# K and Q of the first three chunks in runs of four tokens, turned by f32 identity matmuls, and a new order for the opening

## The chip, the cores and the metric

The kernel runs on one core of a Trainium2 chip. The core has five engines, each with a list of instructions of its own: TensorE (PE, matmuls; its weight loads are shown as PEld), VectorE (DVE), ScalarE (ACT), GpSimd (POOL) and SyncE (SP), which here only issues DMAs. The engines meet through semaphores. Data comes from DRAM into SBUF (128 partitions) by DMA (the page counts 16 DMA engines and shows five queues); matmuls write to PSUM, which the kernel uses as eight banks of 2 KB per partition. The metric is the device time of one execution in microseconds (us), as the median of several runs; lower is better.

## The reference, cut to what matters

Attention with a window of 128 and 4 sink tokens, over 4 batches, 8 heads, 768 tokens and head size 64, then a feed-forward layer that takes the maximum of three products:

```python
scores = (q @ k.T) / sqrt(64)                 # per batch and head
keep = is_sink | ((rel >= 0) & (rel < 128))   # rel = query position - key position
a = exp(where(keep, scores, -1e9) - max); a = a / sum(a)
x = (a @ v)                                   # heads side by side: 3072 x 512
h = maximum(maximum(x @ w1, x @ w2), x @ w3)  # 512 -> 768
out = h @ w_out                               # 768 -> 512, float32
```

## The kernel before, in words

The 3072 tokens are cut into 12 chunks of 256, three to a batch (`CPB = 3`). Eight heads make four pairs (`NP = 4`); two heads of a pair lie on the two halves of the 128 partitions. Every chunk passes these stages, each a small function that is called by name:

- `load` (L76) brings Q, K or V of a chunk in f32 with one DMA on SP. Partition p gets tokens 2p and 2p+1 of all eight heads, so that one run in DRAM is two tokens of one head, 512 bytes. `gate` is a tiny write by POOL into the target that the DMA has to wait for: `pool_gate` writes at once, in POOL's order; `after(wi, c)` copies one number out of weight `wi`, so it waits until that weight has landed, and POOL with it.
- `cast_qk` (L95) casts half of the pairs (group g) to bf16 on a chosen engine, `cast_v` (L104) a quarter of V.
- `turn` and `turn2` (L109, L129) bring the head size onto the partitions: four transposes on TensorE into a bf16 PSUM tile, then one copy to `kT` or `qT` by ScalarE or VectorE. In `turn2`, K and Q of a group share one PSUM bank. From chunk 4 on `turn_dma` does it with DMA transposes on SP. `qT` and `kT` keep even and odd tokens apart (index i), which the masks allow for.
- `premask` writes a mask into a score bank by a matmul, before `score` adds K times Q for a pair; `expo` takes the exponential on ScalarE; `mask` multiplies on VectorE where there was no `premask`. `sink_k`, `sink_v` and `sink_score` do the four sink tokens; `av_open` opens the output banks, `av` multiplies by V and normalises on VectorE, `xpose` (or `xpose_dma`) turns the result.
- `ffn_h(chunk, fp, wi)` is eight matmuls for a third of the hidden size and one of the three weights, followed by a copy (ScalarE, wi = 0) or a maximum (VectorE); `ffn_y` is the last product, `store` the output in runs of two rows (4 KB).
- `load_w` and `load_wo` load the weights from POOL, cast to bf16 on the way. `warm` issues matmuls on zeros whose result nobody uses.

`bank` takes the first of a list of free PSUM banks and `give` puts it at the end, in the order in which the program is written. So a stage can wait for a bank that an earlier one has not yet emptied. Raw tiles have two buffers for each of Q, K and V.

The order is written out by hand: L454 to L655 are the opening, in which chunks 0 to 3 are brought up and the feed-forward of chunks 0 to 2 is woven in, and L656 to L764 are the main loop, in which the feed-forward of chunk i runs beside the attention of chunk i + 1. Every engine takes its instructions in the order of this list. The first `ffn_h` stands at L536.

Of the kernel before, what the change touches and what calls it, by code (L numbers as in the profile page):

```python
# [16 lines left out]
def kernel(  # L17
# [13 lines left out]
    nc = tc.nc  # L31
# [17 lines left out]
    with tc.manual_schedule():  # L49
# [17 lines left out]
        RING = 4  # L67
        kT = [const.tile([128, 2, NP, 2, 64], BF16, name=f"kT{i}") for i in range(RING)]
# [7 lines left out]
        def load(ci, what="kqv", gate=None, part=None, parts=1):  # L76
# [4 lines left out]
            for w in what:  # L81
# [4 lines left out]
                if gate is not None:  # L86
                    gate(dst[0:1, 0, 0, 0:1])
                n = H // parts
# [6 lines left out]
        def cast_qk(ci, w, g, eng):  # L95
# [4 lines left out]
            f = eng.copy if eng is nc.scalar else eng.tensor_copy  # L100
            f(x[:, 2 * g:2 * g + 2].rearrange("q p i a d -> q p a i d"),  # L101
# [7 lines left out]
        def turn(ci, w, g, eng=None):  # L109

            pt = bank([128, 4, 128], BF16, "pt")
# [16 lines left out]

        def turn2(ci, w, g, eng=None):  # L129

            if w == "k":
                pts[ci, g] = bank([128, 2, 4, 128], BF16, "pt")
# [206 lines left out]
        def av(ci, p):  # L339
# [16 lines left out]
            if p == 0:  # L356
# [7 lines left out]
        def xpose(ci, t, eng=None):  # L364
            eng = eng or nc.scalar
            if t == 0:
# [87 lines left out]
        warm(6)  # L454
        load(0, 'k')
        load(0, 'q', gate=pool_gate)
        warm(6)
        masks()
        premask(0, (2,))
        load(0, 'v', gate=pool_gate)  # L460
        cast_qk(0, 'k', 0, nc.gpsimd)
        sink_init()
        cast_qk(0, 'k', 1, nc.vector)
        premask(0, (3,))
        cast_qk(0, 'q', 0, nc.scalar)
        cast_qk(0, 'q', 1, nc.vector)
        turn2(0, 'k', 0, nc.scalar)
        load(1, 'k')
        premask(0, (0,))
        turn2(0, 'k', 1, nc.scalar)  # L470
        turn2(0, 'q', 1, nc.scalar)
        turn2(0, 'q', 0, nc.vector)
        score(0, (0,))
        expo(0, 0)
        load(1, 'q')
        premask(0, (1,))
        sink_k(0)
        cast_v(0, 1, 1, nc.vector)
        load_w(0, 0, 768)
        score(0, (1,))  # L480
        score(0, (2,))
        warm(3)
        cast_qk(1, 'k', 0, nc.vector)
        cast_v(0, 0, 0, nc.vector)
        cast_v(0, 1, 0, nc.gpsimd)
        expo(0, 2)
        expo(0, 1)
        load(1, 'v')
        av_open(0)
        load_w(1, 512, 768)  # L490
        score(0, (3,))
        cast_v(0, 0, 1, nc.vector)
        cast_qk(1, 'q', 1, nc.gpsimd)
        cast_qk(1, 'k', 1, nc.vector)
        av(0, 0)
        expo(0, 3)
        cast_qk(1, 'q', 0, nc.vector)
        turn2(1, 'k', 0, nc.vector)
        load_w(1, 0, 512)
# [156 lines left out]
        for i in range(3, NCH):  # L656
            n, m = i + 1, i - 1
            more = n < NCH
            if i == 3 or i >= NCH - 2:
# [6 lines left out]
                if more:  # L666
                    sink_score(n)
# [140 lines left out]
```

## Time and profile before

| what | us |
|---|---|
| median of 3 runs (179.58 to 180.5) | 179.67 |
| span of the profiled execution, from its first to its last instruction | 179.1 |
| TensorE busy in the span | 170.6 |
| VectorE busy | 125.3 |
| ScalarE busy | 84.6 |
| GpSimd busy | 61.7 |
| first `ffn_h` matmul starts | 18.50 |
| last `ffn_h` of the opening ends, main loop begins | 58.07 |

The page gives no other time for the profiled execution than its span; the 0.57 us between span and median lie outside the first and last instruction. The granted clock of TensorE reads 1.000 over the whole span.

In rows of the timeline the columns are start, duration, engine, line of the kernel, operation, output tile `<-` input tiles, shape, count; the bracket gives the idle time of the engine just before and what ended it. In rows of groups, the numbers behind the bar are busy time, mean ns of one, and idle time before. In rows of windows, behind the length stand the busy times of PE, PEld, DVE, ACT and POOL, with counts of instructions that touch the window, then the granted clock, the busy share of the DMA engines (it can exceed 1 where packets overlap) and GB/s. Bytes of the weights are counted as written, in bf16.

### The profile page before, as it was taken

What the parts mean: (1) busy time and instruction counts of PE and PEld (TensorE: products, weight loads), DVE (VectorE), ACT (ScalarE), POOL (GpSimd) and SP (SyncE); (2) the same over time, 40 slices, a digit from 0 to 9 for tenths busy, and PEclk for the clock granted to TensorE, in tenths of its full rate; (3) what the DMA queues carried; (4) which work ended last, traced back from release to release, by engine and by line L of the source; (5) the groups of instructions that cost most, each with busy time, mean ns of one, the idle gap of its engine ahead of it and who ended that gap; (6) DMA issues with size and microseconds to landing.
All of it is one profiled execution on the core that took longest, in us unless ns stands there. A gap on an engine that the chain in (4) does not pass through costs nothing.

```text
span 179.1 us, 4647 instructions
## 1 busy us (share of the span) xinstructions
PE 170.6 (95%) x1873; PEld 126.8 (71%) x1873; DVE 125.3 (70%) x271; ACT 84.6 (47%) x169; POOL 61.7 (34%) x121
## 2 busy tenths in 40 slices
PE   7789999979999999999999999999999999999991
PEld 2445889746688588598597597696796795796870
DVE  3189752799699797677676775874875875976451
ACT  3386734853772921931824914914716716420210
POOL 4378630161565395066055055146135000000000
PEclk9999999999999999999999999999999999999999
DMA  4999999979999999995998999998999505202203
GB/s 137 290 288 206 249 212 260 225 196 287 326 186 207 294 206 237 226 276 133 243 273 181 249 193 238 239 198 222 262 157 266 40 20 161 117 6 58 117 0 117
DMA packets 69029, 34.90 MB, mean 195 GB/s; under 512 B 26512, under 2 KB 67472, under 8 KB 69008
## 3 DMA queue, kind: packets, MB, share of 16 engines
q1 hardware_dynamic: 64912, 31.33, 81.2%
q0 software_dynamic: 3952, 3.15, 11.1%
q8 instruction: 14, 0.23, 0.5%
q10 hardware_dynamic: 144, 0.13, 0.2%
q14 instruction: 7, 0.06, 0.1%
HBM read 25.17 MB, written 6.29 MB: 176 GB/s over the span
## 4 chain that ended last, share of the span: by engine, by line
PE 86%; DVE 5%; DMA 4%; POOL 1%; issue 1%; ACT 0%; SPq 0%; POOLq 0%
PE h_ps L390 51%; PE y_ps L411 17%; PE o L350 6%; PE st L274 6%; DMA k_raw<-in_k_dram 4%; DVE e_sb L292 2%; PE xt L371 1%; PE pt L115 1%; PE o L332 1%; DVE vb L105 1%; PE sk L300 1%; PE y_ps L421 1%; DVE h_sb L401 1%; DVE k_bf L101 1%; PE pt L137 0%
## 5 line engine op out<-in xcount | busy, mean ns | idle before, releaser
L390 PE MATMUL h_ps<-xT,w 128*128 128x256 bf16 x864 | 101.9, 273 | 0.2 <-DVE h_sb L401 0.2
L390 PEld LDWEIGHTS <-w 128*128 128x128 bf16 x864 | 81.7, 98 | 10.5 <-issue 0.8
L401 DVE TENSOR_TENSOR h_sb<-h_sb,h_ps 128x512 bf16<-128x512 bf16 (+1 forms) x74 | 49.2, 670 | 17.9 <-PE h_ps L390 16.0
L286 ACT ACTIVATE e_sb<-st 128x512 bf16<-128x512 f32 (+1 forms) x96 | 46.2, 578 | 6.4 <-PE st L274 6.3
L397 ACT CAST h_sb<-h_ps 128x512 bf16<-128x512 f32 x36 | 21.1, 587 | 49.2 <-PE h_ps L390 49.0
L105 POOL CAST vb<-v_raw 64x512 bf16<-64x512 f32 x40 | 26.3, 657 | 28.3 <-DMA v_raw<-in_v_dram 24.8
L411 PE MATMUL y_ps<-wo,h_sb 128*128 128x512 bf16 x138 | 32.7, 380 | 1.0 <-DVE h_sb L401 1.0
L292 DVE TENSOR_TENSOR e_sb<-e_sb,msk 128x1024 bf16<-128x1024 bf16 (+1 forms) x42 | 28.9, 720 | 1.5 <-ACT e_sb L286 1.3
L101 POOL CAST k_bf<-k_raw 128x512 bf16<-128x512 f32 x17 | 11.4, 689 | 40.2 <-issue 23.6
L411 PEld LDWEIGHTS <-h_sb 128*128 128x128 bf16 x138 | 12.4, 98 | 15.6 <-DVE h_sb L401 2.0
L358 DVE TENSOR_TENSOR x_sb<-o,rc 128x256 bf16<-128x256 f32 x48 | 20.4, 424 | 1.6
L413 DVE COPY y_sb<-y_ps 128x512 f32<-128x512 f32 x13 | 9.0, 690 | 13.9 <-PE y_ps L411 13.8
L350 PE MATMUL o<-vb,e_sb 128*128 128x65 bf16 x352 | 17.2, 194 | 0.3 <-DVE vb L105 0.2
L350 PEld LDWEIGHTS <-e_sb 128*128 128x128 bf16 x352 | 14.9, 98 | 2.6 <-DVE vb L105 0.4
L274 PE MATMUL st<-qT,kT 64*128 64x128 bf16 (+1 forms) x256 | 14.5, 238 | 0.6 <-DVE qT L141 0.6
L274 PEld LDWEIGHTS <-kT 64*128 64x128 bf16 x256 | 8.3, 94 | 8.1 <-issue 6.2
L355 DVE RECIPROCAL rc<-o 128x4 f32<-128x4 f32 x48 | 8.4, 176 | 4.2 <-PE o L350 4.1
L101 POOL CAST q_bf<-q_raw 128x512 bf16<-128x512 f32 x17 | 10.1, 619 | 3.0 <-DMA q_raw<-in_q_dram 3.0
L413 ACT COPY y_sb<-y_ps 128x512 f32<-128x512 f32 x10 | 5.9, 586 | 7.6 <-PE y_ps L411 7.4
L306 ACT ACTIVATE e_sink<-sk 128x256 bf16<-128x256 f32 x8 | 3.1, 383 | 12.4 <-PE sk L300 12.4
L177 PE MATMUL warm<-wz 128*128 128x512 bf16 x15 | 5.7, 552 | 1.2 <-DVE wz L166 1.2
L101 DVE CAST q_bf<-q_raw 128x512 bf16<-128x512 f32 x5 | 2.6, 525 | 4.6 <-DMA q_raw<-in_q_dram 4.6
(70 smaller groups left out, 72.2 us busy)
## 6 DMA issues: line engine op xcount, KB each, us to landing
k_raw<-in_k_dram SPq DMA_DIRECT2D x12, 512.0 KB, 5.0
q_raw<-in_q_dram SPq DMA_DIRECT2D x12, 512.0 KB, 6.3
v_raw<-in_v_dram SPq DMA_DIRECT2D x12, 512.0 KB, 7.4
out_dram<-y_sb SPq DMA_DIRECT2D x11, 512.0 KB, 3.3
w<-in_moe_w_dram POOLq DMA_DIRECT2D x4, 256.0 KB, 9.0
w<-in_moe_w_dram POOLq DMA_DIRECT2D x1, 768.0 KB, 8.3
wo<-in_moe_w_out_dram POOLq DMA_DIRECT2D x1, 768.0 KB, 11.0
w<-in_moe_w_dram POOLq DMA_DIRECT2D x1, 512.0 KB, 9.2
```

Of the source, the lines that this page charges most:

```text
L101: f(x[:, 2 * g:2 * g + 2].rearrange("q p i a d -> q p a i d"), y[:, 4 * g:4 * g + 4].rearrange("q (p a) i d -> q p a i d", a=2))
L105: eng.tensor_copy(vb[ci % RING][64 * i:64 * i + 64, n, :, 0:D], raws[ci, "v"][64 * n:64 * n + 64, :, i])
L274: nc.tensor.matmul(st[a][:, s:s + q1 - q0].rearrange("q n (i r) -> q n i r", i=2), lhsT=x[hp, n, p].rearrange("q i r -> q (i r)"), rhs=qc[ ...
L286: nc.scalar.activation(e[:, a, lo:], st[a][:, lo:], AF.Exp, scale=scale)
L292: (eng or nc.vector).tensor_mul(e[:, :, lo:], e[:, :, lo:], msk0 if lo else msk)
L350: nc.tensor.matmul(o[:, t, a], lhsT=e[:, a, s], rhs=vb[cv % RING][:, n, 2 * p + a], start=first, stop=True, skip_group_check=True)
L358: nc.vector.tensor_mul(xs[ci][:, :, p], o[:, :, :, 0:D], rc.unsqueeze(3).to_broadcast([128, 2, 2, D]))
L390: nc.tensor.matmul(hp[:, f].rearrange("q (i t r) -> q i t r", i=2, t=2), lhsT=w_sb[wi][:, ds, c0:c0 + 128], rhs=xTs[ci][:, :, ds].rearrang ...
L397: nc.scalar.copy(dst, hp)
L401: nc.vector.tensor_max(dst[:, x], dst[:, x], hp[:, x])
L411: nc.tensor.matmul(yp, lhsT=hs[ci][:, fb, t * 128:(t + 1) * 128], rhs=wo[:, fb], start=(fb == 0), stop=(fb == FB - 1))
L413: (nc.scalar.copy if eng is None else eng.tensor_copy)(ys[ci][:, t], yp)
```

## The change: what it does

For chunks 0 to 2 (`QUAD = 3`, the whole first batch) K and Q are loaded by two DMAs each. DMA x brings heads 4x to 4x+3 onto the partitions 2p + x, four tokens to a partition, so that a run in DRAM is four tokens of one head, 1024 bytes. `cast_qk` reads the other layout. `turn` and `turn2` hand over to `turn4`: four matmuls against the identity, whose outputs go into an f32 PSUM tile with steps in the address, so that the tokens come out in the layout that `kT` and `qT` had before, and then one copy. Each turn has a bank of its own. V, and Q and K from chunk 3 on, are as before.

The opening is the same set of calls in another order, with other engines for some of the casts and copies, and with 8 and 5 warm matmuls in place of 6, 6 and 3. In the new list every one of the first eight turns copies on ScalarE, `masks_late` comes early on POOL, Q of chunk 1 is loaded ahead of K, the last third of w2 right behind that of w1 and ahead of the rest of w1. The main loop is written in four branches without the tests on `more`. `av` and `xpose` allocate their tile at whichever call comes first.

```diff
+        QUAD = 3
@@ in load
+                if ci < QUAD and w != "v":
+                    for x in range(2):
+                        nc.sync.dma_start(
+                            out=dst.rearrange("(p x) h i d -> x p (h i d)", x=2)[x]
+                                .rearrange("p (h e) -> p h e", h=4),
+                            in_=src[b, 4 * x:4 * x + 4, t0:t0 + 256]
+                                .rearrange("h (p i) d -> p h (i d)", i=4))
+                    continue
@@ in cast_qk
+            if ci < QUAD:
+                f(x[:, 2 * g:2 * g + 2].rearrange("q u v a d -> q (u v) a d"),
+                  y[:, 4 * g:4 * g + 4].rearrange("q (a u) v d -> q (u v) a d", a=2))
+                return
@@ in turn and turn2
+            if ci < QUAD:
+                return turn4(ci, w, g, eng)
@@ new
+        def turn4(ci, w, g, eng=None):
+            pt = bank([128, 2, 2, 2, 32, 2], F32, "pt")
+            x = bfs[ci, w]
+            for i in range(4):
+                y = x[:, 2 * g + i // 2, i % 2].rearrange("s a d -> s (a d)")
+                if w == "q":
+                    o = pt[:, :, i % 2, :, :, i // 2].rearrange("q x n r -> q n r x")
+                else:
+                    o = pt[:, :, :, i % 2, :, i // 2].rearrange("q x n r -> q n r x")
+                nc.tensor.matmul(o, lhsT=y, rhs=ident, start=True, stop=True)
+            eng = eng or (nc.scalar if w == "q" else nc.vector)
+            f = eng.copy if eng is nc.scalar else eng.tensor_copy
+            if w == "q":
+                f(qT[ci % RING].rearrange("q (x p) i n r -> q p x (i n r)", x=2)[:, g],
+                  pt.rearrange("q x i n r j -> q x (i n r j)"))
+            else:
+                f(kT[ci % RING].rearrange("q n (x p) i r -> q p x n (i r)", x=2)[:, g],
+                  pt.rearrange("q x n i r j -> q x n (i r j)"))
+            give(pt)
```

The new list, up to the main loop, on one line for each few calls (calls on several engines, in program order):

```python
load(0,'k'); load(0,'q',gate=pool_gate); masks(); load(0,'v',gate=pool_gate); warm(8); premask(0,(3,))
cast_qk(0,'k',1,nc.scalar); sink_init(); cast_qk(0,'k',0,nc.gpsimd); turn2(0,'k',0,nc.scalar); load(1,'q')
turn2(0,'k',1,nc.scalar); masks_late(); premask(0,(1,)); load_w(0,0,768); cast_qk(0,'q',1,nc.vector)
load(1,'k'); cast_qk(0,'q',0,nc.vector); turn2(0,'q',1,nc.scalar); turn2(0,'q',0,nc.scalar)
score(0,(1,)); score(0,(3,)); load_w(1,512,768); load_w(2,512,768); load(1,'v'); premask(0,(0,))
cast_v(0,1,0,nc.vector); score(0,(0,)); expo(0,1); expo(0,3); load_w(1,0,512); cast_v(1,1,0,nc.gpsimd); warm(5)
...
premask(0,(2,)); av_open(0); expo(0,0); cast_qk(1,'q',1,nc.scalar); cast_qk(1,'q',0,nc.vector); score(0,(2,))
expo(0,2); sink_k(0); cast_qk(1,'k',0,nc.vector); turn2(1,'q',0,nc.scalar); cast_qk(1,'k',1,nc.vector); av(0,3)
sink_v(0); turn2(1,'k',0,nc.scalar); load(2,'k',gate=after(0,300)); av(0,1); av(0,2); load_w(2,0,256)
turn2(1,'q',1,nc.scalar); load(3,'q',gate=after(0)); turn2(1,'k',1,nc.scalar); av(0,0); score(1,(2,)); score(1,(0,))
expo(1,2); cast_qk(2,'q',0,nc.gpsimd); mask(1,2); premask(1,(1,)); load(2,'v',gate=after(1)); xpose(0,0,nc.scalar)
load_w(2,256,512); expo(1,0); score(1,(1,)); load_wo(); xpose(0,1,nc.vector); ...; sink_score(1); score(1,(3,))
expo(1,1); ffn_h(0,2,0); mask(1,0); expo(1,3); ffn_h(0,0,0); cast_qk(2,'k',1,nc.gpsimd); av_open(1)
cast_v(2,1,1,nc.gpsimd); cast_v(2,1,0,nc.gpsimd); load(3,'k',gate=after(1)); av(1,2); av(1,0); av(1,1); av(1,3)
load(3,'v',gate=after(2)); ffn_h(0,1,0); ffn_h(0,2,1); ...; cast_qk(3,'q',1,nc.gpsimd); load(4,'q',gate=pool_gate)
...
turn(2,'k',1,nc.vector); turn(2,'k',0,nc.scalar); ffn_h(0,0,1); sink_score(2); score(2,(2,)); score(2,(0,)); expo(2,2)
cast_qk(3,'q',0,nc.scalar); score(2,(1,)); score(2,(3,)); mask(2,2); expo(2,1); ffn_h(1,0,2); mask(2,1); ffn_h(1,2,2)
expo(2,0); ffn_h(1,1,1); ffn_h(0,1,2); turn(3,'q',1,nc.scalar); expo(2,3); mask(2,0); ffn_h(1,1,2); cast_v(2,0,1,nc.gpsimd)
av_open(2); cast_qk(3,'k',0,nc.gpsimd); cast_qk(3,'k',1,nc.gpsimd); turn(3,'q',0,nc.scalar); load(4,'v')
load(5,'k',gate=pool_gate); av(2,2); mask(2,3); av(2,0); ffn_y(1,0,nc.vector); ffn_y(0,0); turn(3,'k',0,nc.scalar)
...
expo(3,1); load(4,'k',gate=after(2)); ...; store(0); ...; load(5,'q'); ...; turn_dma(4,'q'); turn_dma(4,'k')
...
```

More of the change, by code (lines that the diff above doesn't have):

```diff
@@ L656 @@
         for i in range(3, NCH):
             n, m = i + 1, i - 1
[L658 to L661 removed]
+            if i == 3:
+                sinks(n)
                 load(i + 3)
```

539 lines of the change are left out of this document (294 added, 245 removed).

## The prediction

> **What bounds the kernel now.** I read the page's header and chain first, then the busy windows of its stages, then the timeline of the entry, then what moved the DMA.
>
> ```profile
> span 179.1 us, 4647 instructions
> PE 170.6 (95%) x1873; PEld 126.8 (71%) x1873; DVE 125.3 (70%) x271; ACT 84.6 (47%) x169; POOL 61.7 (34%) x121
> ...
> PE 86%; DVE 5%; DMA 4%; POOL 1%; issue 1%; ACT 0%; SPq 0%; POOLq 0%
> ```
>
> The chain is TensorE nearly everywhere, so time can be won only where TensorE idles or does filler. The windows say where that is.
>
> ```profile
> 0.00:18.50 18.50, 15.09 (x152) 7.86 (x152) 11.24 (x36) 10.51 (x22) 11.68 (x33) 1.00 1.04 230
> 18.50:58.07 39.57, 38.23 (x448) 30.44 (x448) 30.47 (x66) 22.00 (x44) 15.75 (x33) 1.00 1.13 239
> 58.07:164.80 106.73, 106.73 (x1198) 79.97 (x1198) 77.61 (x161) 49.96 (x100) 34.31 (x56) 1.00 0.94 189
> ...
> L177 PE MATMUL warm<-wz 128*128 128x512 bf16 x15 | 5.7, 552 | 1.2 <-DVE wz L166 1.2
> ```
>
> Cuts: the first `ffn_h` starts at 18.50, the main loop at 58.07. The loop is 100% busy to 164.8 and its work is untouched, so a shift of its start passes through to the end. Lost are 18.50 - 15.09 = 3.4 us of idle and 5.7 us of warm matmuls before 18.50 (**entry**), and 39.57 - 38.23 = 1.34 us after it (**middle**). At most these 10.5 us can be won, and some 5 of them pass before K has landed at all.
>
> The entry, from the timeline (start, duration, engine, line, count, in brackets the idle time before it and its releaser):
>
> ```profile
> 0.75 0.46 SPq L90 DMA_DIRECT2D k_raw<-in_k_dram  x1
> 1.20 4.90 PE L177 MATMUL warm<-wz 128*128 128x512 bf16 x12 [1.20 <-DVE wz L166]
> 5.08 0.43 DVE L101 CAST k_bf<-k_raw 128x512 bf16<-128x512 f32 x1 [1.31 <-DMA k_raw<-in_k_dram]
> 5.19 0.79 POOL L101 CAST k_bf<-k_raw 128x512 bf16<-128x512 f32 x1 [2.23 <-DMA k_raw<-in_k_dram]
> 6.58 0.39 PE L137 MATMUL pt<-ident,k_bf 128*128 128x128 bf16 x4
> 6.89 0.43 DVE L101 CAST q_bf<-q_raw 128x512 bf16<-128x512 f32 x1 [1.38 <-DMA q_raw<-in_q_dram]
> 6.95 0.62 ACT L101 CAST q_bf<-q_raw 128x512 bf16<-128x512 f32 x1 [4.70 <-DMA q_raw<-in_q_dram]
> 7.47 1.06 ACT L144 COPY kT<-pt 128x512 bf16<-128x512 bf16 x2
> 8.59 0.61 PE L137 MATMUL pt<-ident,q_bf 128*128 128x128 bf16 x8 [1.07 <-ACT kT L144]
> 9.24 0.90 POOL L239 DMA_DIRECT2D w<-in_moe_w_dram  x1
> 10.14 3.29 ACT L286 ACTIVATE e_sb<-st 128x384 bf16<-128x384 f32 x8 [0.55 <-PE st L274]
> 12.41 0.70 POOL L101 CAST q_bf<-q_raw 128x512 bf16<-128x512 f32 x1 [0.89 <-DMA q_raw<-in_q_dram]
> 15.52 2.06 ACT L286 ACTIVATE e_sb<-st 128x512 bf16<-128x512 f32 x4 [1.16 <-PE st L274]
> 15.53 1.29 POOL L210 TENSOR_SCALAR msk<-addm 128x512 bf16<-128x512 bf16 x2
> 16.91 1.14 POOL L212 TENSOR_SCALAR msk<-addm 128x384 bf16<-128x384 bf16 x2
> 17.94 0.29 PE L332 MATMUL o<-vs,e_sink 32*128 32x130 bf16 x8
> 18.50 1.05 PE L390 MATMUL h_ps<-xT,w 128*128 128x256 bf16 x8
> ```
>
> K of chunk 0 lands at 5.05, Q at 6.88, 1.83 later; Q of chunk 1 at 12.4. TensorE stands 1.07 before the Q transposes, because they share a PSUM bank with K's copies. Exps start at 10.14 only.
>
> DMA (last two columns: share, GB/s), then its issues, the last column being us to landing:
>
> ```profile
> 3.00:13.00 10.00, 8.12 (x72) 4.10 (x71) 4.98 (x15) 5.02 (x12) 4.68 (x12) 1.00 1.20 298
> 166.50:167.00 0.50, 0.50 (x7) 0.44 (x6) 0.29 (x1) 0.00 (x0) 0.00 (x0) 1.00 1.01 410
> ...
> w<-in_moe_w_dram POOLq DMA_DIRECT2D x1, 768.0 KB, 8.3
> wo<-in_moe_w_out_dram POOLq DMA_DIRECT2D x1, 768.0 KB, 11.0
> ```
>
> From 3 to 13 us the queue runs the six loads of chunks 0 and 1, in runs of 512 B, at 298 GB/s: 524 KB / 298 = 1.76 us each. The first weight, issued at 9.24, lands 8.3 later, at 17.5, behind them. The `out` store (runs of 4 KB) goes at 410 GB/s, 1.28 us per 512 KB.
>
> **The change part by part.** *Loads.* K and Q of chunks 0 to 2 go in runs of 1 KB, each as two DMAs on alternate partitions: six more issues on SP at up to 0.46. SP waits for gates in between, so this costs nothing unless the second half starts late: it is issued at 1.2, and a load moves for 1.76, and its half is wanted only after the first half's 0.88. The price of a 1 KB run has no row. Bounds: 1.76 us per load (as now) and 1.28 (as 4 KB runs). Through both points, per engine: 512 B take 512 x 16 / 298 = 27.5 ns, 4 KB take 160 ns, so 18.9 ns per 512 B and 8.6 fixed; 1 KB makes 46.4 ns, 353 GB/s, 1.49 us. I take 1.5, which is also nearer the 512 B end. That is 0.27 for each load: K0 lands at 4.8, Q0 at 6.3, V0 (unchanged) at 8.1, Q1 9.6, K1 11.1, V1 12.9, and the queue is free for weights 1.1 us sooner.
>
> The Trainium skill ("DMA: Bandwidth & Descriptors", Why small descriptors are slow) puts the loss at about 3 cycles a packet beside one per 32 B; by that estimate 1 KB gives 35/38 of the time, 1.62 us, and Q0 would land at 6.6. No row here shows cycles.
>
> *Casts, transposes.* As many casts of as many elements: nothing. `turn4` makes four identity matmuls of 128 columns where four transposes stood; the rows of these are 0.39 for four. New are a 4-byte output and a stepped PSUM address; no row has the step. Bounds: 55 ns each as now (a gain is excluded: a column a cycle is what they do now), or double, +0.22 per turn. I take no change, since every matmul into PSUM here already writes f32 (`st`, `h_ps`) at its column rate. The copy out reads f32 instead of bf16:
>
> ```profile
> L397 ACT CAST h_sb<-h_ps 128x512 bf16<-128x512 f32 x36 | 21.1, 587 | 49.2 <-PE h_ps L390 49.0
> L144 ACT COPY kT<-pt 128x512 bf16<-128x512 bf16 x3 | 1.6, 583 | 0.3 <-PE pt L137 0.3
> L413 DVE COPY y_sb<-y_ps 128x512 f32<-128x512 f32 x13 | 9.0, 690 | 13.9 <-PE y_ps L411 13.8
> L122 DVE COPY kT<-pt 128x512 bf16<-128x512 bf16 x1 | 0.4, 418 | 0.0
> ```
>
> On ScalarE 587 against 583: nothing. On VectorE 690 against 418, +0.27, but the new order leaves VectorE only one of the twelve (`turn(2,'k',1)`), with two `ffn_h` behind it as cover; uncovered it costs the 0.27. ScalarE gets the others: 11 x 0.53 back to back.
>
> *Entry, new order.* Warm 8 instead of 12 plus 5 instead of 3: 8 x 0.41 from 1.2 ends at 4.5, and two pre-masks follow. K0 at 4.8: POOL cast 0.79 to 5.6, four matmuls 0.39 to 6.0, the two ScalarE copies 1.06 to 7.1. Q0 at 6.3: two VectorE casts 0.43 to 7.2; matmuls under the second; the copies run from 7.2 to 8.3 (own banks, so the 1.07 wait is gone). Now ScalarE is the chain without a gap: three exps of chunk 0 (3.29/4 = 0.82 each) to 10.8, cast Q1 0.62 to 11.4, fourth exp to 12.2, four copies 4 x 0.53 to 14.3 (K1 landed 11.1, cast by 12.1), exp of chunk 1 (2.06/2 = 1.03) to 15.4, `xpose` copy to 15.9, half an exp 0.52 to 16.5, which frees the bank of the first `ffn_h`. The weight must be there: 17.5 - 1.1 = 16.4, and its issue does not slip, as POOL's `masks_late` (1.29 + 1.14) moves ahead of it but `sink_init` and the casts it loses make room (5.6 + 2.4 = 8.0 against 9.24). First `ffn_h` at 16.8 with 0.3 for semaphores, against 18.50: **-1.7**. VectorE's casts and `av` products go under ScalarE (VectorE is 11.24 busy in 18.50 now, and gives a cast to ScalarE).
>
> *Middle.* Same matmuls, plus `av_open(1)`, 0.3 by the row at 17.94, which stood before 18.50. A wait is added: `expo(1,3)` stands on ScalarE behind half an exp, the sink's exp (some 0.4 by its size), `expo(1,1)` and an `h` copy (16.5 + 0.52 + 0.4 + 1.03 + 0.59 + 1.03 = 20.1), while TensorE reaches `av(1,3)` at 19.4 (two `ffn_h`, `av_open`, three short `av`): 0.7 idle, with all that follows queued behind. The middle's price of an `ffn_h` (from the chain) and its one long wait (from the timeline) now:
>
> ```profile
> 23.88 4.41 PE h_ps L390 x40
> ```
>
> ```profile
> 39.89 0.61 PE L411 MATMUL y_ps<-wo,h_sb 128*128 128x512 bf16 x2 [0.99 <-DVE h_sb L401]
> ```
>
> An `ffn_h` is 4.41/5 = 0.88. The 0.99 is VectorE late with masks and maxes of chunk 2; the new order has the same ones, a mask after each exp between maxes, and I leave half, 0.5. Then the loads that feed this stage, issue and first use:
>
> ```profile
> 20.30 0.37 SPq L90 DMA_DIRECT2D q_raw<-in_q_dram  x1
> 30.47 0.43 DVE L101 CAST q_bf<-q_raw 128x512 bf16<-128x512 f32 x1 [3.21 <-DMA q_raw<-in_q_dram]
> ...
> 25.84 0.37 SPq L90 DMA_DIRECT2D v_raw<-in_v_dram  x1
> 35.22 0.61 POOL L105 CAST vb<-v_raw 64x512 bf16<-64x512 f32 x1 [8.47 <-DMA v_raw<-in_v_dram]
> ...
> 36.10 0.37 SPq L90 DMA_DIRECT2D k_raw<-in_k_dram  x1
> 40.19 0.61 POOL L101 CAST k_bf<-k_raw 128x512 bf16<-128x512 f32 x1 [1.51 <-DMA k_raw<-in_k_dram]
> ```
>
> Beside weights a 512 B load needs 5 us of queue (Q2 issued 20.30, landed 30.4; V2 after it 35.2, 9.4 from its issue). If the queue alternates by run, Q2 and K2 in larger runs clear sooner, and the weights a little later. In the new order `load(3,'q')` stands ahead of V2 on SP, V2's gate waits on POOL for w1 (about 26, as its issue at 25.84 now), and on POOL the casts of V2 stand ahead of the gate of K3 and the casts of K3. By the same 9.4 V2 would land at 35.4; I take 1 off for the larger runs before it. With V2 at 34.4 POOL has cast two of its parts at 35.7, K3 is issued at 36.2, lands 4.1 later (as 36.10 to 40.19), and is cast two times 0.61 on, 41.5. TensorE comes to `av(2,2)` at 16.8 + 18 x 0.88 + 4.5 of short groups + 0.7 = 37.8 and wants all V2 casts, the last of which POOL ends near 38.3, so 0.5, the same time in which VectorE is late; then two `ffn_y` and it wants K3, at 41.4: even. Idle in the middle 0.7 + 0.5 + 0.3 for the rest = 1.5. So 38.23 + 0.3 + 1.5 = 40.0 against 39.57: **+0.4**.
>
> *Loop, tail.* The flattened branches issue the same work in the same order: nothing. On SP K5 goes ahead of K4, `store(0)` and `turn_dma(4)` behind both; K4 waits for K3's buffer (cast at 41.5, so landed near 46) and its transposes land by about 56, wanted at 57: nothing, but up to 1 us if they slip.
>
> Sum: -1.7 + 0.4 = -1.3. Span 179.1 to 177.8; the median 179.67 stands 0.57 above the span: **178.4**.
>
> **Rivals.** (a) *Runs of 1 KB win nothing*: the halves take as long as the whole. For: one set of 16 engines, already at share 1.20. Against: 410 GB/s for 4 KB. Then Q0 lands at 6.9, ScalarE's chain starts 0.6 later, K1 (12.4) adds 0.3, first `ffn_h` at 17.7: -0.8 + 0.4, 179.3. The Trainium skill ("DMA: Bandwidth & Descriptors", Rules for kernel authors) says so of two transfers to partition halves: do not bother, they share the engines; it does not weigh the longer run.
>
> (b) *Slower: POOL's queue head.* V2 lands late, POOL stands at its cast, and K3's gate and casts stand behind it. Each us that V2 is late is a us for TensorE at `turn(3,'k',0)`, and `wo`, issued behind the same gate near 27 and 11.0 under way, is wanted at 38. For: V2 took 9.4 us now. Against: larger runs clear Q2 and K2 sooner. V2 at 36.6 instead of 34.4 costs 2.2, 180.6, from where it is slower; at 37.5 it is 181.5.
>
> (c) *The stepped f32 write is slow.* At double, 4 turns of the entry's path 0.9 and 16 matmuls of chunk 2 x 55 ns 0.9: 180.2. For: no row has it. Against: f32 writes at full rate elsewhere.
>
> (d) *Middle without the 0.7 at `av(1,3)` and half of the rest*: 178.4 - 1.1 = 177.3. For: it holds only if ScalarE comes a little sooner.
>
> **How the numbers follow.** Forecast 0.45 (its own range 177.6 to 179.0), (a) 0.18, (b) 0.22, (c) 0.07, (d) 0.08. About 0.5% (0.9 us, as far as the three runs spread) is what can be told from no change: faster holds (d) and 0.42 of the forecast, 0.50; same its other edge, (a) and 0.03 of (c), 0.24; slower (b) and the rest of (c), 0.26. The range leaves out a tenth each way: 177.2 to 180.8.
>
> **What would show it.** Right: Q0's first cast at 6.3, 353 GB/s in the first 10 us, ScalarE unbroken from 7 to 16, first `ffn_h` near 16.8, four identity matmuls in 0.39, loop near 56.8. Wrong: 298 GB/s (a); POOL idle before V2's cast past 36 and TensorE idle before `turn(3,'k',0)` (b); identity matmuls of over 0.6 for four (c); a first `ffn_h` held by the weight instead of ScalarE.

## The result, and the profile after

The changed kernel takes 185.46 us (median of 4 runs, 184.56 to 186.72) against 179.72 for the kernel before beside it (179.58 to 180.5): the ratio is 1.031, with a 95% interval of 1.025 to 1.037. The prediction of 178.4, between 177.2 and 180.8, is wrong, and so is its sign. Ratios leave disturbed executions out and medians do not (three of ten in e19 and six of ten in e21 fall out so); where no interval is given below, too few undisturbed ones were left.

In this kernel and in before an execution's time stands 1.7 to 1.9 us above its own span, not 0.57: the profiled execution of before (span 179.1) was one of its longer ones, and the median span of those run later is 178.1. So the predicted span of 177.8, taken as it stands, would have meant about 179.6, no change; the predicted gain of 1.3, taken off the usual span, would have meant 178.6.

First the page of the kernel after (span; busy times; granted clock by slices of 4.6 us; the chain by engine), then its stages as windows, cut at the first `ffn_h` (23.09) and at the start of the loop (64.20):

```profile
span 184.9 us, 4639 instructions
PE 173.1 (94%) x1859; PEld 129.9 (70%) x1871; DVE 121.5 (66%) x263; ACT 88.6 (48%) x177; POOL 62.0 (34%) x121
...
PEclk9999759999999999999999999999999999999999
...
PE 85%; DMA 6%; POOL 3%; SPq 2%; issue 1%; ACT 1%; DVE 0%; POOLq 0%
```

```profile
0.00:23.09 23.09, 15.33 (x141) 8.57 (x141) 10.91 (x33) 12.83 (x27) 12.79 (x36) 0.96 0.96 216
23.09:64.20 41.11, 40.92 (x444) 32.76 (x444) 27.52 (x61) 22.76 (x46) 15.07 (x31) 0.94 0.94 216
64.20:170.90 106.70, 106.22 (x1189) 79.90 (x1197) 77.06 (x160) 50.85 (x102) 34.18 (x56) 1.00 0.89 187
```

The loop is what it was: 106.7 us. The entry is 4.6 us longer (23.09 against 18.50) and the middle 1.5 longer (41.11 against 39.57), though TensorE idles only 0.2 us in it, against 1.3 before; its mean clock is 0.94. The waits and the timeline show where the entry went. Waits read: who waited for whom, us in total, times, longest.

```profile
PE sk L338 <- POOL ks L268: 3.9, 1, 3.9
PE pt L154 <- DVE q_bf L111: 1.9, 1, 1.9
```

```profile
2.21 1.27 SPq L91 DMA_DIRECT2D q_raw<-in_q_dram  x2
4.17 1.68 SPq L91 DMA_DIRECT2D q_raw<-in_q_dram  x2
...
5.56 1.05 PE L154 MATMUL pt<-ident,k_bf 128*128 128x128 bf16 x8 [0.69 <-POOL k_bf L111]
...
5.90 1.64 SPq L91 DMA_DIRECT2D k_raw<-in_k_dram  x2
7.58 0.74 SPq L99 DMA_DIRECT2D v_raw<-in_v_dram  x1
...
8.33 0.97 DVE L111 CAST q_bf<-q_raw 128x512 bf16<-128x512 f32 x2 [4.50 <-DMA q_raw<-in_q_dram]
8.81 1.15 PE L154 MATMUL pt<-ident,q_bf 128*128 128x128 bf16 x8 [1.88 <-DVE q_bf L111]
...
13.02 0.61 PE L154 MATMUL pt<-ident,q_bf 128*128 128x128 bf16 x4
14.57 0.59 ACT L161 CAST kT<-pt 128x512 bf16<-128x512 f32 x1
...
18.96 0.42 DVE L118 CAST vb<-v_raw 64x512 bf16<-64x512 f32 x1 [0.39 <-DMA v_raw<-in_v_dram]
19.06 2.47 POOL L118 CAST vb<-v_raw 64x512 bf16<-64x512 f32 x3 [7.59 <-DMA v_raw<-in_v_dram]
...
21.74 0.42 POOL L268 COPY ks<-kT 64x16 bf16<-64x16 bf16 x2
...
22.21 0.41 PE L338 MATMUL sk<-qT,ks 128*32 128x256 bf16 x4 [3.86 <-POOL ks L268]
```

K of chunk 0 comes at 4.85 as predicted, Q at 8.3 instead of 6.3. Four identity matmuls take 0.61, not 0.39. The large loss is further on: V of chunk 1 (V1 below) is first cast at 18.96. POOL, idle for 7.6 us by then, stands at its cast; behind its three casts stands `sink_k(0)` (L268), behind that `sink_score(1)` on TensorE (L338), and behind that the first `ffn_h`. In the kernel before, POOL made the sink keys ahead of its first weight load, and V1 came in time:

```profile
8.67 0.45 POOL L230 COPY ks<-kT 64x16 bf16<-64x16 bf16 x2 [1.95 <-ACT kT L144]
...
14.16 1.28 POOL L105 CAST vb<-v_raw 64x512 bf16<-64x512 f32 x2 [0.25 <-DMA v_raw<-in_v_dram]
...
17.15 0.29 PE L300 MATMUL sk<-qT,ks 128*32 128x256 bf16 x4
```

In the changed kernel TensorE waits 3.9 us, and then its clock is halved for 6.8 us. These windows are the last one before the clock falls and the stretch for which it stays down:

```profile
17.81:21.23 3.42, 0.54 (x4) 0.05 (x1) 2.17 (x4) 1.10 (x3) 2.08 (x3) 1.00 1.36 203
21.23:28.06 6.83, 5.84 (x55) 3.84 (x56) 0.41 (x2) 3.52 (x7) 1.81 (x7) 0.50 0.93 185
```

Half the clock from 23.09 to 28.06 costs an estimated 2.5 us of matmul time. So 3.9 of wait and 2.5 of clock are a little more than the 6.1 that entry and middle lost. This is the longest of the four executions, with a mean granted clock of 0.982; the other three have 0.990 and 0.991, so about half as long at half clock.

The DMA rows, before and then after (DMA share and GB/s last), show both sides of the larger runs:

```profile
4.00:7.00 3.00, 3.00 (x16) 1.44 (x15) 0.54 (x2) 0.05 (x1) 1.47 (x6) 1.00 1.21 297
7.00:12.00 5.00, 3.34 (x35) 1.72 (x33) 2.83 (x6) 3.97 (x9) 2.62 (x5) 1.00 1.21 290
```

```profile
4.00:7.00 3.00, 2.24 (x14) 1.19 (x12) 0.00 (x0) 1.41 (x3) 1.87 (x4) 1.00 0.73 225
7.00:12.00 5.00, 3.06 (x26) 1.67 (x27) 2.93 (x6) 2.82 (x8) 4.34 (x6) 1.00 1.10 331
```

From 7 to 12 us the queue moves 331 GB/s instead of 290, near the 353 predicted. From 4 to 7 it moves 225 instead of 297, with a DMA share of 0.73 instead of 1.21. By 12 us the packet records of both kernels count the same bytes, 5.3 of the six loads.

### The profile page after: what moved, and what is told of

Same layout as the page of the kernel before. It is cut to its first block, busy times and chain, and to the rows that moved or that the text cites. A ratio compares the mean times of both kernels' runs of the same rounds, so it can differ in the third digit from the quotient of the medians.

```text
span 184.9 us, 4639 instructions
## 1 busy us (share of the span) xinstructions
PE 173.1 (94%) x1859; PEld 129.9 (70%) x1871; DVE 121.5 (66%) x263; ACT 88.6 (48%) x177; POOL 62.0 (34%) x121
## 4 chain that ended last, share of the span: by engine, by line
PE 85%; DMA 6%; POOL 3%; SPq 2%; issue 1%; ACT 1%; DVE 0%; POOLq 0%
PE h_ps L428 52%; PE y_ps L449 16%; PE o L388 6%; DMA v_raw<-in_v_dram 6%; PE st L312 5%; SPq L91 2%; PE o L370 1%; PE pt L154 1%; POOL vb L118 1%; PE sk L338 1%; PE xt L409 1%; PE y_ps L459 1%; PE pt L130 1%; ACT e_sb L324 0%; POOL addm L236 0%
## 5 line engine op out<-in xcount | busy, mean ns | idle before, releaser
L428 PEld LDWEIGHTS <-w 128*128 128x128 bf16 x864 | 83.0, 99 | 11.2 <-issue 0.6
L439 DVE TENSOR_TENSOR h_sb<-h_sb,h_ps 128x512 bf16<-128x512 bf16 (+1 forms) x74 | 49.3, 671 | 20.8 <-PE h_ps L428 19.3
L118 POOL CAST vb<-v_raw 64x512 bf16<-64x512 f32 x39 | 25.5, 653 | 23.7 <-DMA v_raw<-in_v_dram 22.2
L449 PE MATMUL y_ps<-wo,h_sb 128*128 128x512 bf16 x126 | 31.7, 380 | 0.6
L330 DVE TENSOR_TENSOR e_sb<-e_sb,msk 128x1024 bf16<-128x1024 bf16 (+1 forms) x42 | 27.6, 688 | 2.4 <-ACT e_sb L324 2.3
L449 PEld LDWEIGHTS <-h_sb 128*128 128x128 bf16 x138 | 12.5, 98 | 14.6 <-issue 1.6
L451 DVE COPY y_sb<-y_ps 128x512 f32<-128x512 f32 x14 | 9.7, 690 | 14.4 <-PE y_ps L449 14.3
L312 PE MATMUL st<-qT,kT 64*128 64x128 bf16 (+1 forms) x256 | 14.5, 240 | 0.1
L114 POOL CAST q_bf<-q_raw 128x512 bf16<-128x512 f32 x15 | 9.1, 634 | 3.0 <-DMA q_raw<-in_q_dram 3.0
L451 ACT COPY y_sb<-y_ps 128x512 f32<-128x512 f32 x9 | 5.3, 589 | 4.9 <-PE y_ps L449 4.7
L338 PE MATMUL sk<-qT,ks 128*32 128x256 bf16 x32 | 2.4, 292 | 3.9 <-POOL ks L268 3.9
L215 PE MATMUL warm<-wz 128*128 128x512 bf16 x13 | 4.6, 513 | 1.2 <-DVE wz L204 1.2
```

The lines of the kernel that those rows point to most:

```text
L118: eng.tensor_copy(vb[ci % RING][64 * i:64 * i + 64, n, :, 0:D], raws[ci, "v"][64 * n:64 * n + 64, :, i])
L312: nc.tensor.matmul(st[a][:, s:s + q1 - q0].rearrange("q n (i r) -> q n i r", i=2), lhsT=x[hp, n, p].rearrange("q i r -> q (i r)"), rhs=qc[ ...
L330: (eng or nc.vector).tensor_mul(e[:, :, lo:], e[:, :, lo:], msk0 if lo else msk)
L428: nc.tensor.matmul(hp[:, f].rearrange("q (i t r) -> q i t r", i=2, t=2), lhsT=w_sb[wi][:, ds, c0:c0 + 128], rhs=xTs[ci][:, :, ds].rearrang ...
L439: nc.vector.tensor_max(dst[:, x], dst[:, x], hp[:, x])
L449: nc.tensor.matmul(yp, lhsT=hs[ci][:, fb, t * 128:(t + 1) * 128], rhs=wo[:, fb], start=(fb == 0), stop=(fb == FB - 1))
```

## The experiments

Times are medians; the kernel before took 179.8 to 180.1 beside each of these runs. "V1 lands" is the start of the first cast that waited for it, in the profiled execution. The diffs show the telling lines alone.

**What stands behind V1: e1_sink_first, e2_warm.** e1 moves one call, so that POOL makes the sink keys before it comes to V1's casts:

```diff
         load_w(0, 0, 768)
+        sink_k(0)
...
-        sink_k(0)
```

> The changed kernel with one call moved: sink_k(0) stands on POOL right behind the first weight instead of behind the three casts of chunk 1's V. Theory P (POOL's queue: sink_score(1) waits 3.9 us for sink_k, which waits behind casts that wait for V1, and TensorE then runs at half clock from 21 to 28): sink_score(1) near 18.3, first ffn_h near 18.9 instead of 23.1, granted clock 1.00 throughout, time about 180, that is 5 us less than the changed kernel. Theory L (the new loads and turns are what costs): the wait moves on to av(1), which needs the same V casts, and at most 2 us come back, 183 or more.

Measured: 180.54, ratio 1.003 (0.9996 to 1.006).

```profile
18.63 1.92 PE L428 MATMUL h_ps<-xT,w 128*128 128x256 bf16 x16
19.46 2.55 POOL L118 CAST vb<-v_raw 64x512 bf16<-64x512 f32 x3 [7.84 <-DMA v_raw<-in_v_dram]
```

V1 is as late as in the changed kernel, yet the first `ffn_h` starts at 18.63 and the clock stays whole. So 4.9 of the 5.7 us come from the place of this one call behind a late transfer. e2 leaves the order and fills TensorE's wait:

```diff
+        warm(18)
         sink_score(1)
```

> The changed kernel with 18 warm matmuls (3.9 us) in TensorE's list right ahead of sink_score(1), where it stands idle. The wait for POOL stays. If the half clock after the idle time costs what the windows show (4.8 us of work at half speed), 2.4 us less than the changed kernel, 183; first ffn_h stays near 23, granted clock 1.00. If the clock falls for another reason than the idle time, no change.

Measured: 184.91, ratio 1.026 (1.019 to 1.034), 183.59 at its lowest. The clock stays whole behind the wait, but only 0.6 us come back in the median, and the intervals overlap. In the profiled execution the 18 matmuls end at 23.9, 1.1 us after the keys are there: they were too many, and the half clock's own price is not isolated by this run.

**Half of the change at a time: e3_order_only, e4_layout_only.** e3 sets `QUAD = 0` in the new order, and each turn has a bank of its own; e4 puts the new loads and `turn4` into the old order.

> The new order with the old layout: all loads in runs of 512 bytes, all turns as transposes into bf16, each with its own bank. Theory P with the early weights as the cause of the late V1: V1 still lands past 17, TensorE still waits about 3 us before sink_score(1), and the time is about 183 to 184. Theory L (half loads are slow to start, so that V1 comes last): Q0 is back at 6.9, V1 near 14, no wait, time 178 to 179.5.

> The old order with the new loads, casts and turns for chunks 0 to 2. Measured in the changed kernel: Q0 lands at 8.3 instead of 6.9, and four identity matmuls take 0.60 instead of 0.39. Theory L: +1.4 us in the entry and 0.2 for each of the eight turns of chunk 2 and half of the rest, 181 to 182.5. Theory P: the layout alone costs under 1 us, 180 to 180.7.

Measured: e3 180.01, ratio 1.0005 (0.998 to 1.003); e4 181.82, ratio 1.011 (1.008 to 1.014). The order alone neither wins nor loses; V1 lands at 14.2 in it. (The profiled execution of e3, 182.48, is the longest of its ten, with the clock halved from 8.3 to 15.1.) The layout alone loses 2 us; there V1 lands at 15.1, and the sink keys stand ahead of its casts.

**Why V1 is late: e8_weights_behind_v1, e9_two_dmas_512, e5_side_halves.** e8 issues the first four weight loads behind POOL's first cast of V1. e9 is e3 with each K and Q load of chunks 0 to 2 cut in two by heads, still in runs of 512 B on all partitions. e5 is e1 with the halves on partitions 0 to 63 and 64 to 127 instead of alternate ones.

```diff
 e9
+                np_ = 2 if ci < 3 and w != "v" else parts
+                n = H // np_
+                for g in range(np_):
 e5
+                            out=dst[64 * x:64 * x + 64].rearrange("p h i d -> p (h i d)")
```

> The changed kernel with the first four weight DMAs issued by POOL only behind its first cast of chunk 1's V. If V1 is late because it shares the DMA with the weights, it lands near 14, sink_score(1) does not wait for POOL any more, and the first ffn_h now waits for the weight, near 23 to 24. If V1 is late by its own place in the queue, it still lands past 17.

> e3_order_only with K and Q of chunks 0 to 2 loaded by two DMAs each, by heads, on all 128 partitions, runs of 512 bytes. If cutting a load in two is what makes it slow to start, Q0 lands at 7.4 or later and V1 past 16, and the time is 0.5 to 1 us above e3_order_only. If not, Q0 at 6.9, V1 at 14.2, time 180.0.

> e1_sink_first with the two halves of a load on partitions 0 to 63 and 64 to 127 instead of on alternate ones; runs of 1 KB, two DMAs and four tokens to a partition stay, and the matmuls' outputs now step by 8 bytes in their inner loop instead of jumping by 1 KB. If the alternate partitions make the loads slow to start: DMA share over 1 from 4 us on, Q0 at 6.4 to 6.9, V1 near 13 to 14, time 178.5 to 179.5. If it is the two DMAs: Q0 past 7.4, V1 past 17, time 180 to 180.9. If the jump by 1 KB doubled the matmuls: four take 0.39; if it is the f32 output or any step: 0.60.

Measured: e8 186.69 (one run), with V1 at 14.6; e9 187.55, ratio 1.043 (1.037 to 1.049), V1 at 20.7; e5 183.2, ratio 1.018 (1.013 to 1.022), 210 GB/s from 4 to 7 us and 237 from 7 to 12. In e8 the same loads bring V1 in time with no weights beside them, though in one execution alone; its time is no better, since POOL then issues weights ahead of `sink_k(0)` and the first `ffn_h` comes at 22.4. In e9 POOL also issued its first weight a us earlier (7.06), so it does not isolate the cut. Halves on neighbouring partitions are worse than alternate ones.

The DMA view by single microseconds shows how weights hold V1 back. Rows: q0 is the weights, q1 SP's loads; packets, MB, share of 16 engines. The changed kernel in 13 to 14, 15 to 16 and 17 to 18 us:

```profile
q0 software_dynamic: 124, 0.19, 104.3%
q1 hardware_dynamic: 62, 0.03, 14.7%
...
q0 software_dynamic: 129, 0.20, 108.7%
q1 hardware_dynamic: 28, 0.01, 6.8%
...
q0 software_dynamic: 348, 0.19, 134.3%
q1 hardware_dynamic: 8, 0.00, 1.9%
```

At 14 us 97 records of V1 are left (40, 28, 13, 8 and 8 in the five microseconds to 19): 90 of its 1024 packets, and the end records of 7 of the 16 engines. Those engines now alternate with weights. The records name no engine, but those between 16.8 and 17.9 us come at one step and can be read as the last engine's: a 512-byte packet each 152 ns, where such a packet takes 27 to 41 ns in the kernel before:

```
start us  16.805 16.956 17.108 17.260 17.412 17.564 17.715 17.867
```

The last weight packets of 1.5 KB start at the same step, between them; from 18 us on, beside weight packets of 512 bytes, the step is 76 ns. By an estimate from these figures an engine that is 25 packets behind when the weights begin comes in 4 us late instead of 0.8. The Trainium skill ("DMA: Bandwidth & Descriptors", Queues, rings and completion order) says that each engine goes round its queues packet by packet, with some 9 to 17 descriptors to a packet. That the queues take turns agrees with these starts; the size of a turn does not, if each record is one descriptor, since single records stand 152 ns apart.

**Late issue or uneven engines: e14_v1_ahead_of_k1, e16_two_queues, e18_old_loads_late_v1, e20_quad_chunk0_only.** e14 is the changed kernel with `load(1,'v')` ahead of `load(1,'k')`; e16 is e1 with the second halves of chunks 0 and 1 issued from ScalarE, and chunk 1's loads issued at the start; e18 is e3 with V1 held by a gate until POOL's masks are done (its call stands ahead of the first weight's, K1's too); e20 is the changed kernel with `QUAD = 1`, and whole loads for chunks 1 and 2.

```diff
 e16
-                        nc.sync.dma_start(
+                        (nc.scalar if x and ci < 2 else nc.sync).dma_start(
 e18
+        load(1, 'v', gate=pool_gate)
         load_w(0, 0, 768)
```

> The changed kernel with one edit: V of chunk 1 is loaded ahead of K of chunk 1 instead of behind it (SP issues it near 5.9 instead of 7.6); sink_k(0) stays behind V1's casts on POOL. Theory, V1 falls behind the weights because the halves push its issue late: V1 lands near 12 to 13, POOL's casts of V1 start there instead of at 19.1, the sink's scores do not wait, no half clock follows, 180.0 to 181.0. Rival, POOL's own order is the cause whatever V1 does (its casts of 2.5 us and the weight issues stand ahead of sink_k(0)): the wait stays above 2 us, 183 or more. Rival, K1 takes V1's bad place: K1 lands after 15 and its casts hold VectorE and the turns, the same 183 or more with the wait at the turns.

> e1_sink_first (180.5) with the second half of each K and Q load of chunks 0 and 1 issued from ScalarE's queue instead of SP's, and the loads of chunk 1 issued at the start. Theory, SP's issues starve the queue: 4 to 7 us go from 232 to about 300 GB/s, Q0 is cast near 6.3 instead of 7.5, V1 lands near 13, TensorE's work ahead of the loop is 1 us earlier, 179 to 179.7. Rival, single packets stall whoever issues: Q0 stays at 7.3 to 8.3, V1 between 14 and 19 by chance, 180 to 181.

> e3_order_only (180.0, whole loads in runs of 512 B) with V of chunk 1 issued behind POOL's masks, near 8.4 instead of 6.8. If a late issue is what sends the last load behind the weights: V1 lands at 18 or later, TensorE waits over 3 us at the sink's scores, 183 or more. If the cause is in the 1 KB halves themselves: V1 lands at 14.2 as in e3, 180.0.

> The changed kernel with the runs of 1 KB and the identity matmuls for chunk 0 alone; chunks 1 and 2 are loaded whole in runs of 512 B and transposed as before. If the halves of chunk 1, right ahead of V1, leave engines behind: V1 lands at 13.5 to 14.5, no wait at the sink's scores, 179.3 to 180.3. If those of chunk 0 are enough: V1 at 16 or later, the wait above 2 us, 183 or more.

Measured: e14 185.24 (4 runs, 182.28 to 185.96); e16 182.1, ratio 1.012 (1.008 to 1.017); e18 180.46, ratio 1.003 (0.9996 to 1.006); e20 187.83, ratio 1.043 (1.040 to 1.047). One line of each carries the verdict, of e14, e16, e18 and e20 in this order:

```profile
17.34 0.76 DVE L111 CAST k_bf<-k_raw 128x512 bf16<-128x512 f32 x2 [4.82 <-DMA k_raw<-in_k_dram]
```

```profile
4.00:7.00 3.00, 2.53 (x14) 1.29 (x12) 0.00 (x0) 1.31 (x3) 1.84 (x3) 1.00 1.01 326
...
20.42 2.55 POOL L118 CAST vb<-v_raw 64x512 bf16<-64x512 f32 x3 [8.36 <-DMA v_raw<-in_v_dram]
```

```profile
8.53 0.37 SPq L99 DMA_DIRECT2D v_raw<-in_v_dram  x1
...
14.12 1.92 POOL L118 CAST vb<-v_raw 64x512 bf16<-64x512 f32 x3 [2.50 <-DMA v_raw<-in_v_dram]
```

```profile
4.00:7.00 3.00, 2.81 (x14) 1.29 (x12) 0.00 (x0) 1.36 (x3) 1.84 (x3) 1.00 0.79 216
...
24.49 0.41 PE L318 MATMUL sk<-qT,ks 128*32 128x256 bf16 x4 [6.17 <-POOL ks L248]
```

In e14 (its longest execution) V1 is in time (13.2) and K1 takes its place at 17.3: the last load loses, whichever it is, and the theory that V1's own late issue did it falls. In e16 the second issuing queue fills the 4 to 7 us (326 GB/s), and V1's last engine still ends at 20: SP's slow issue was real, and not the cause. Nor did it bring Q0, which came at 9.1, later than in the changed kernel, with the loads of chunk 1 under way beside it. In e18 V1 is issued a us later than in the changed kernel, in the old runs, and lands at 14.1. In e20 the halves of chunk 0 alone leave the queue at 216 GB/s; then the whole of V1 is still to come when the weights begin, and TensorE waits 6.2 us; its time is the worst of all. The packet records add what the views average over. Long packets are those of over 0.2 us between 3 and 13 us; each engine's part of a load ends with a 4-byte record, from which its last columns come (when 1, 14 and all 16 engines are done with chunk 1's last load):

| kernel | long packets | longest, us | weights begin | 1 done | 14 done | 16 done |
|---|---|---|---|---|---|---|
| before | 0 | - | 12.8 | 12.8 | 13.4 | 13.5 |
| e18 (old runs, V1 issued late) | 0 | - | 12.8 | 12.8 | 13.3 | 13.4 |
| after | 12 | 0.51 | 12.3 | 12.7 | 16.1 | 18.6 |
| e1 | 24 | 1.10 | 11.9 | 12.7 | 15.7 | 19.1 |
| e8 (no weights beside it) | 22 | 1.24 | 16.8 | 12.5 | 13.7 | 14.0 |
| e19 (loads as e1) | 18 | 1.14 | 12.3 | 12.3 | 13.1 | 18.6 |
| e6 (loads as e1) | 14 | 0.51 | 12.2 | 12.2 | 13.2 | 14.1 |
| e10 (loads as e1) | 17 | 0.96 | 12.2 | 12.2 | 13.4 | 14.4 |
| e16 | 5 | 0.83 | 11.8 | 12.0 | 13.1 | 20.0 |
| e20 | 16 | 1.09 | 11.5 | 19.3 | 20.2 | 20.9 |
| e9 (512 B, two DMAs) | 4 | 0.99 | 10.4 | 18.6 | 19.5 | 20.3 |

Whole loads in runs of 512 B have no long packet after 3 us and keep the 16 engines within 0.7 us; every kernel with its loads cut in two has some, of up to 1.2 us in this table, and its engines drift apart.

The drift alone does not make V1 late. e6 and e10, two kernels of the next group, have the loads of e1 and issue their first weight at 8.2 and 8.3, as e1 does at 8.0; in their profiled executions V1 was complete at 14.1 and 14.4:

```profile
14.50 1.94 POOL L118 CAST vb<-v_raw 64x512 bf16<-64x512 f32 x3 [2.65 <-DMA v_raw<-in_v_dram]
...
14.76 1.94 POOL L118 CAST vb<-v_raw 64x512 bf16<-64x512 f32 x3 [2.42 <-DMA v_raw<-in_v_dram]
```

What divides the 20 profiled executions is when the weights begin. In eight of them no weight packet moved before the first engine was done with chunk 1's last load, and all 16 engines were done with it by 13.4 to 14.5. In the other twelve weights began earlier, by 0.04 us (e19) to 8.2 us (e9), and the load ended at 15.1 to 20.9. So with half loads V1 may come in time or not. The order of issue does not decide it: in e18 the first weight was issued at 8.45 and V1 at 8.53, and no weight moved until 12.8. What lets the weights in early is not shown, nor why the packets of half loads stall: e9 has few long ones and was still late, with weights that began 2 us earlier, and runs of 1 KB in one whole DMA were not tried.

**The stepped write: e6_f32_unstepped, e10_no_step, e19_no_step_warm.** e6 is e1 with the four outputs one behind the other in f32; e10 is e1 with bf16 transposes without a step, the step being taken by the copies out of PSUM (K's in two instructions); e19 adds seven warm matmuls between the turns of K and Q of chunk 0.

```diff
 e6
+                o = pt.rearrange("q a b c r j -> q (a b c r j)")[:, 128 * i:128 * i + 128]
 e10
+                nc.tensor.transpose(o, y, ident)
 e19
         turn2(0, 'k', 1, nc.scalar)
+        warm(7)
```

> e1_sink_first with the outputs of the identity matmuls written one behind the other, in f32, as 128 columns without a step (the tokens then come out in a wrong order, so the scores are of other tokens; everything else is as before). If the step doubled the price, four matmuls take 0.39 and the time falls by some 0.5 to 1 us; if f32 output against the identity does it, 0.60 and no change.

> e1_sink_first (180.5) with the runs of 1 KB kept, but turned by transposes whose output in PSUM is contiguous bf16; the copies out of PSUM do the step instead. The four transposes should take 0.39 instead of 0.60, 12 turns x 0.21 = 2.5 us of TensorE in all, of which 4 turns' worth (0.8) lies on the entry's path and up to 1.7 in the middle. If the step was what was left of the loss: 178.5 to 179.5. If the copies, now reading bf16 at a step of two and K's in two instructions, take the gain back on ScalarE (over 700 ns for a turn instead of 590): 180 to 181.

> e10_no_step (181.8) with seven warm matmuls between the turns of K and Q of chunk 0, where TensorE idles. If its loss was the half clock from 8.4 to 15 us: clock 1.0 there, 179.3 to 180.0. If the copies of K in two instructions and the stepped reads were the loss: 181.5 or more.

Measured: e6 180.68 (2 runs, 179.14 and 182.22); e10 181.81, ratio 1.010 (1.008 to 1.013), slower than e1; e19 180.25, ratio 0.998 (0.994 to 1.003), with executions from 178.92 to 182.22. Of e6 a turn, then of e10 three windows of 3.41 us or twice that (PE busy first, the clock third from the end), and of e1 the window at the same place:

```profile
14.49 0.39 PE L155 MATMUL pt<-ident,q_bf 128*128 128x128 bf16 x4
```

```profile
4.85:8.26 3.41, 1.61 (x16) 0.79 (x14) 0.79 (x2) 1.76 (x5) 3.12 (x5) 1.00 0.94 277
8.26:15.09 6.83, 5.90 (x31) 2.15 (x29) 3.58 (x8) 4.08 (x9) 4.28 (x8) 0.50 1.12 288
15.09:18.50 3.41, 3.11 (x66) 2.52 (x63) 2.35 (x9) 3.25 (x9) 2.54 (x7) 1.00 1.31 199
```

```profile
4.95:8.36 3.41, 1.72 (x13) 1.03 (x12) 0.84 (x2) 1.51 (x3) 3.06 (x6) 1.00 0.92 270
```

Four matmuls into f32 take 0.39 without the step, so the step raises the price (to 0.61), not the f32. Eight behind each other take 1.05 with it and took 0.61 before, so each further one costs 110 ns instead of 55. Taking the step away made the kernel slower: TensorE, waiting for Q, was busy for 1.61 of the 3.41 us to 8.26, and then its clock was halved for 6.83 us; e1, at 1.72, kept it. With warm matmuls in the gap the clock stays at 1.0 and 1.6 us come back. How busy is busy enough, these runs do not say: e9 kept the clock after such a window with 1.65 us busy, e6 lost it for 3.41 us after one with 1.70, and e3 for 6.83 us after one with 1.84. The Trainium skill ("TensorE: Matmul & The Clock Gate", Part 1) gives windows of 3413 ns that run freely, and an idle window as the condition for half rate. The lengths agree (3.41 and 6.83); the condition does not, as windows that were busy for about half were enough here.

**Mends together: e13_order_sink_first, e15_all_three, e17_two_queues_no_step, e21_chunk0_no_step_warm.** e13 is e3 with e1's move; e15 is e10 with V1 ahead of K1; e17 is e16 with e10's turns; e21 is e19 with `QUAD = 1`.

> The new order alone with the loads and transposes of before (e3_order_only, 180.0), and sink_k(0) on POOL right behind the first weight's issue as in e1_sink_first. If sink_k(0)'s place matters only where V1 is late: 180.0, no change, since V1 lands at 14 there. If POOL's casts still hold the sink a little in that order: 179.3 to 179.7.

> All three mends together: sink_k(0) early on POOL, no step in PSUM, V of chunk 1 loaded ahead of K of chunk 1. If the three causes found are the whole loss, what is left is the gain of 1 KB runs, some 1 us at the entry: 178 to 179, faster than before. If the larger runs win nothing once the start is lost to the twelve DMAs of half a load, 179.7 to 180.3, and K1 landing after 14 holds the turns of chunk 1.

> e16_two_queues with the contiguous transposes of e10_no_step (181.8). If Q0 comes a us earlier, TensorE does not idle long enough to lose its clock, and the 0.21 per turn is won: 178.3 to 179.3. If Q0 stays at 7.5, the clock is at half from 8.4 to 15 as in e10: 181.5 to 182.

> e19_no_step_warm (180.25, lowest 178.9) with the 1 KB layout for chunk 0 alone, so that V1 should come in time in each execution: 178.7 to 179.5 and a spread under 1 us. If the gain of e19's best executions came from chunk 1's larger runs, 179.7 to 180.3.

Measured: e13 180.07, ratio 1.001 (0.999 to 1.003); e15 183.27, 1.017 (1.014 to 1.021); e17 182.48, 1.012 (1.006 to 1.018), with one of its four executions at 437.48, which nothing here explains; e21 183.18, 1.004 (1.001 to 1.008), with executions from 180.34 to 186.59. In the longest of these, the profiled one, V1 was still late (21.1). The profiled executions of e15 and e17 lost their clock for 3.41 us from near 10 on. None beats the kernel before: by medians e3 and e13 come nearest, and the lowest executions of e19 (178.92) and e6 (179.14) are too few to call a gain. e13 shows what bounds the entry once its order is free of waits:

```profile
18.81 0.22 PEld L408 LDWEIGHTS <-w 128*128 128x128 bf16 x3 [1.01 <-DMA w<-in_moe_w_dram]
18.81 0.39 PE L408 MATMUL h_ps<-xT,w 128*128 128x256 bf16 x2 [0.79 <-ACT e_sb L304]
```

The first `ffn_h` starts at 18.81: its weight has only then landed, and the exp that frees its bank ends at about the same time, so here neither alone would bring it much sooner.

## Why the prediction was wrong, point by point

- **Loads, "1.49 us each".** In the steady stretch the runs of 1 KB went at 331 GB/s, against 353 forecast and 290 before. The step failed at the start: "costs nothing unless the second half starts late" was the condition, and a half cost SP 0.63 to 0.70 (pairs of 1.27 and 1.41) instead of up to 0.46. The estimate of 1.62 us for a load that the prediction worked out from the Trainium skill ("DMA: Bandwidth & Descriptors", Why small descriptors are slow), 324 GB/s, was nearer to the 331. The queue ran at 225 GB/s from 4 to 7 us, Q0 came 2.0 us late, and by 12 us nothing was won. The slow issue is not all of it: in e16 the queue ran at 326 GB/s there, and Q0 came later still.
- **"V1 12.9".** This is the failed step that decided. 12.7 is when the first engine was done; the last was done at 18.6. A landing was reckoned as bytes over GB/s, the mean of 16 engines, and the weights were taken to start behind V1, as they do before (12.82, the first engine being done with V1 at 12.81). Here they began at 12.3, ahead of that. Neither the uneven engines nor the price of a packet beside weights (152 ns against 27 to 41) was in the sum, though the 9.4 us of V2 beside weights stood in the working.
- **POOL's queue head.** Rival (b) had the mechanism, a late V with POOL standing at its cast and TensorE's next need behind it, but sought it at V2 and K3; the place was V1 and `sink_k(0)`, which the new order moves from ahead of the first weight load to behind V1's casts; the working put this move at nothing, without a reason. e1 prices it at 4.9 us. This and the landing of V1 are the two halves of the miss.
- **Identity matmuls at 55 ns each.** Rival (c), the double price, was right: 110 ns each behind another instead of 55, 0.61 for four against 0.39. Its 1.8 us are not borne out: e19, without the step, stands 0.3 below e1 in the medians, within the intervals, but it has other copies and more warm matmuls as well; e6 changes the step alone, and its two executions decide nothing.
- **Copies.** ScalarE's f32 copies took 0.53 back to back and 0.59 singly, as forecast.
- **Entry "-1.7".** Measured +4.6; with the one call moved +0.1 (18.63), and in e19 -0.3 (18.21). ScalarE's copies of Q0 began at 9.5 instead of 7.2 (9.0 in e1, 8.3 in e19), with Q0, and "the weight must be there: 16.4" was wrong as well: it landed near 18.8 in e13. Three more weight loads were issued right behind it there and moved beside it, which may be why; no run isolates this.
- **Middle "+0.4", with waits of 1.5.** Measured +1.5, with idle of 0.2 and a clock of 0.94; the predicted waits did not come, and 2.5 us of half clock did. Without it the middle would by this estimate be 0.9 shorter than before.
- **Loop: nothing.** 106.7 in both; right.
- **Rival (a), that larger runs win nothing,** came true as an outcome in e1 and e19, though the rate did rise: the start took back what it won.

## What to carry to other kernels

A transfer lands with the slowest of its engines: where a load ends close to the start of another stream on the same engines, a lag of a few packets can be multiplied by that stream's packets, in one execution and not in another, so leave a margin there or put nothing urgent behind that load. Before a call is moved on a queue, ask what each wait ahead of it would cost if it came 5 us late, and keep small producers that TensorE needs (here 0.4 us of sink keys) ahead of casts that wait for DMA. Work that looks idle, a slow matmul or a warm one, can be what holds the clock: in e10 less work cost more time, as the stretch of half clock behind it outweighed the matmul time that was saved.

## What the runs showed of the hardware that was not expected

- A matmul of 128 columns whose f32 output goes to PSUM with a step takes 110 ns behind another instead of 55 (eight 1.05 us against 0.61); four take 0.60 to 0.61 against 0.39 without the step (e6, e10), with the step of the change as with that of e5.
- The clock falls behind windows of 3.41 us in which TensorE is busy too little, not only idle: windows with 1.61 (e10), 1.70 (e6) and 1.84 us (e3) of busy time lost it, others with 1.65 (e9) and 1.72 (e1) kept it, so busy time alone does not tell. It came back after 3.41 (e6) or 6.83 us (e10, e3, the changed kernel).
- On one DMA engine, as the records are read above, a 512-byte packet that shares with weight packets of 1.5 KB comes every 152 ns, against 27 to 41 ns for such a packet in the kernel before.
- Chunk 1's last load was complete by 14.5 us in all eight profiled executions in which no weight packet moved before its first engine was done; where weights began sooner, it was complete at 15.1 to 20.9 in all twelve.
- The first half loads (64 partitions, 256 KB) cost SP 0.63 to 0.70 us each to issue, the first three whole ones of before 0.37 to 0.46. From 7 to 12 us halves on neighbouring partitions moved 237 GB/s (e5), alternate ones 327 in e1 and 331 in the changed kernel, with 291 (e2) as the lowest of all kernels that have them for three chunks.
